# Seven filling matmuls instead of thirteen ahead of the first inverse transform, and two of four weight differences on GpSimd

## The chip, the cores and the metric

The kernel runs on one core of a Trainium2 chip. The core has a matrix engine (TensorE, PE in the profile, with its weight loads as PEld), VectorE (DVE), ScalarE (ACT), GpSimd (POOL) and SyncE (SP, used here only to issue transfers), and 16 DMA engines. The metric is the time of one execution in microseconds on the device, the median of several.

## What is computed

A spectral filter along the sequence, followed by a feed-forward layer with a squared ReLU:

```
X = rfft(x, axis=1)                  # x: 8 x 3008 x 256
y = irfft(X * (filt_r + i filt_i))   # 1505 frequencies x 256 channels
t = y.reshape(24064, 256)
h = max(t @ w_in, 0)                 # w_in:  256 x 2048
out = (h * h) @ w_out                # w_out: 2048 x 256
```

Inputs and output are float32; inside the kernel matmuls take float16 and accumulate in float32.

## The kernel before, in words

**The transform** of each of the 8 sequences is a product of 3008 = 64 x 47 points and takes four matmul steps. `unit_a` makes the 47-point transforms (result u, written to DRAM as dU). `read_u` brings it back turned (ut). `unit_b` makes the 64-point step, and VectorE multiplies it with the filter (prod, L421). For sequences 1 to 7 GpSimd then issues two DMAs per piece that add the swapped half to the other (L429). `unit_p` makes the first inverse step (ze, written to DRAM as dZ). `read_z` reads a quarter of it back as z: two DMAs, one per half of the partitions, into one of two z tiles that take turns (L479). `unit_y` makes the last inverse step: four matmuls (L497), and a copy of PSUM to yt by ScalarE (L504) or VectorE (L506). yt holds channels by tokens.

**The feed-forward layer** works on 47 groups of 512 tokens. The main loop runs over slots s, 8 per group. In each slot `ffn_g1` makes two hidden tiles of 128 x 512 of group g (eight matmuls at most, L527) and ScalarE applies the ReLU (L531); every second slot VectorE squares four tiles (L538).

The second matmul of group g - 1 goes on in the same slots. All groups but the last use seven products of half-size blocks instead of eight. With h cut into a11, a12, a21, a22 (even and odd hidden tiles, first and second half of the tokens) and W_out into b11, b12, b21, b22 (even and odd hidden tiles, left and right 128 columns), `sums` makes four sums of blocks of h per group on VectorE (L613, L616, L619, L622), and `make_t` makes, once in the kernel, four differences of the blocks of W_out, each 128 x 1024 in float16:

- T0 = b12 - b11, used by product 5
- T1 = b22 - T0, used by product 6
- T2 = b22 - b12, used by product 7
- T3 = b21 - T1, used by product 4

`products` spreads the seven products over eight slots (the table PARTS) and collects them in two PSUM tiles psX and psY (matmuls L642). Copies by ScalarE and additions by VectorE (L657, L663) finish the two halves "top" and "bot" of the output, and SyncE stores them.

**The order of work.** Each engine runs its instructions in the order in which the program issues them; the order is written out by hand. In the main loop a slot issues, one after the other: `ffn_g1` of the group, transform units that `fft_plan` puts there, the differences, the products of the group before, more units, the sums, the square, and the stores. Products of group 0 begin in slot 9.

**Around the change.** The prologue handles sequence 0 alone. Its last lines (L790 to L805) read the first two quarters of z. GpSimd copies one element of the first quarter (`tiny`, L793), which makes it wait for z; only then does it issue the two loads of W_out (`load_wout`, L321; 8 of 16 hidden tiles each, turned to float16 on the way). TensorE goes through the 47-point steps of sequence 1 (`unit_a`, L347), whose results SyncE writes to dU (L330), and then through the filling matmuls (L800): products of a zero tile with a constant into a PSUM tile that nothing reads. After them come the first four pieces of `unit_y` (with two zero matmuls each, L495) and the main loop.

The queues that matter here are SyncE's, which holds in this order the writes of dZ, the reads of two quarters of z, the eight writes of dU, the read of z's third quarter (L805), and the read of ut; and GpSimd's, which holds `tiny`, the two loads of W_out, and then nothing until the first DMAs of L429.

Of the kernel before, what the change touches and what calls it, by code (L numbers as in the profile page):

```python
# [110 lines left out]
def kernel(  # L111
# [9 lines left out]
    nc = tc.nc  # L121
# [35 lines left out]
    def psF(name):  # L157
        return pps.tile([128, 512], F32, tag="psF", name=name, bufs=2)
# [316 lines left out]
    def read_z(b, c, ks=(0, 1)):  # L475
        zt = ztiles[c % 2]
        v = dZ[b].rearrange("(q j) d -> q j d", j=NM)
        for k in ks:
            nc.sync.dma_start(out=zt[64 * k:64 * k + 48],  # L479
                              in_=v[48 * k:48 * k + 48, 8 * c:8 * c + 8, :])  # L480
        zts[(b, c)] = zt
# [29 lines left out]
    def ffn_g1(g, s):  # L511
        if s == 0:
            h2s[g] = p_h2.tile([128, NJT, TG], F16, tag="h2", name=f"h2_{g}")
        h2 = h2s[g]
        ps = psH(f"psH_{g}_{s}")
        segs = []
        t = g * TG
        while t < (g + 1) * TG:
            b, r = divmod(t, S)
            n = min((g + 1) * TG - t, S - r)  # L520
            segs.append((t - g * TG, b, r, n))
            t += n
        for i in range(2):
            jt = 2 * s + i
            for o, b, r, n in segs:
                for dt in range(2):
                    nc.tensor.matmul(ps[:, i, o:o + n],  # L527
                                     sWin[:, dt, jt * 128:(jt + 1) * 128],
                                     yts[b][:, dt, r:r + n],
                                     start=(dt == 0), stop=(dt == 1))  # L530
        nc.scalar.activation(out=h2[:, 2 * s:2 * s + 2, :], in_=ps, func=AF.Relu)  # L531

    def ffn_sq(g, s):
        n = 1 if g == NG - 1 else 2
        if (s + 1) % n:
            return
        v = h2s[g][:, 2 * (s + 1 - n):2 * s + 2, :]
        nc.vector.tensor_mul(out=v, in0=v, in1=v)  # L538

    def ffn_g2(g, s):  # L540
        t, half = divmod(s, 2)
        if s % 4 == 0:
            pso[g] = psO(f"psO_{g}_{s}")
        elif g == NG - 1 and half == 0:
            pso[g] = psF(f"psO_{g}_{s}").rearrange("p (a d) -> p a d", d=256)
        for jt in range(8 * half, 8 * half + 8):
            nc.tensor.matmul(pso[g][:, t % 2, :], h2s[g][:, jt, t * 128:(t + 1) * 128],  # L547
                             sWout[:, jt, :], start=(jt == 0), stop=(jt == NJT - 1))

    def ffn_out(g, s):  # L550

        step = 1 if g == NG - 1 else 2
        if (s + 1) % (2 * step):
            return
        n = s // 2 + 1 - step
        ost = p_out.tile([128, 2, 256], F32, tag="ost", name=f"ost_{g}_{s}")
        h0 = n % 2
        nc.scalar.copy(out=ost[:, h0:h0 + step, :], in_=pso[g][:, h0:h0 + step, :])
        store(g, n, step, ost)
# [25 lines left out]
    def make_t(k):  # L585

        w = sWout.rearrange("p (q e) c -> p q e c", e=2)
        b11, b12 = w[:, :, 0, 0:128], w[:, :, 0, 128:256]
        b21, b22 = w[:, :, 1, 0:128], w[:, :, 1, 128:256]
        if k == 0:  # L590
            sg["t"] = p_t.tile([128, 4, 8, 128], F16, tag="t", name="sT")
        t = sg["t"]
        i0, i1 = ((b12, b11), (b22, t[:, 0]), (b22, b12), (b21, t[:, 1]))[k]
        nc.vector.tensor_sub(out=t[:, k], in0=i0, in1=i1)
        sg["w"] = {1: b11, 2: b21, 3: b22, 4: t[:, 3], 5: t[:, 0], 6: t[:, 1], 7: t[:, 2]}

    def quads(g):
# [3 lines left out]
    def sums(g, k):  # L601

        if k not in (0, 1, 2, 4):
            return
        a11, a12, a21, a22 = quads(g)
        if k == 0:
            sg[g] = {1: a11, 2: a12, 4: a22}
        f = sg[g]
        if k in (0, 2):
            f["s"] = p_x32.tile([128, 2, 8, D], F16, tag="x32", name=f"sum_{g}_{k}")  # L610
        t = f["s"][:, 0 if k in (0, 2) else 1]
        if k == 0:
            nc.vector.tensor_add(out=t, in0=a21, in1=a22)  # L613
            f[5] = t
        elif k == 1:
            nc.vector.tensor_sub(out=t, in0=f[5], in1=a11)  # L616
            f[6] = t
        elif k == 2:
            nc.vector.tensor_sub(out=t, in0=a11, in1=a21)  # L619
            f[7] = t  # L620
        else:
            nc.vector.tensor_sub(out=t, in0=a12, in1=f[6])  # L622
            f[3] = t
# [7 lines left out]
    def products(g, k, s):  # L631

        f = sg[g]
        for p, m0, m1 in PARTS[k]:
            if p == 1 and m0 == 0:
                f["x"] = psO(f"psX_{g}").rearrange("p a (t c) -> p a t c", t=2)
            if p == 2 and m0 == 0:
                f["y"] = psO(f"psY_{g}").rearrange("p a (t c) -> p a t c", t=2)
            o = f["x"][:, 0] if p in (1, 6, 7, 4) else f["y"][:, 0 if p == 2 else 1]
            for m in range(m0, m1):  # L640
                q, t = divmod(m, 2)
                nc.tensor.matmul(o[:, t, :], f[p][:, q, 128 * t:128 * t + 128], sg["w"][p][:, q, :],  # L642
                                 start=(m == 0 and p in (1, 2)), stop=(q == 7),
                                 skip_group_check=True)
            if m1 < 16:
                continue
            if p == 1:
                f["top"] = p_out.tile([128, 2, 256], F32, tag="ost", name=f"top_{g}")
                nc.scalar.copy(out=f["top"][:, :, 0:128], in_=o)
            elif p == 6:  # L650
                nc.scalar.copy(out=f["top"][:, :, 128:256], in_=o)
            elif p == 7:
                f["bot"] = p_out.tile([128, 2, 256], F32, tag="ost", name=f"bot_{g}")
                nc.scalar.copy(out=f["bot"][:, :, 128:256], in_=o)
            elif p == 2:
                for v, i in ((f["top"][:, :, 0:128], 0), (f["bot"][:, :, 128:256], 1)):
                    nc.vector.tensor_add(out=v, in0=f["y"][:, i], in1=v)  # L657
            elif p == 4:
                nc.scalar.copy(out=f["bot"][:, :, 0:128], in_=o)
                stores.append((s + 1, g, 2, f["bot"]))  # L660
            elif p == 3:
                v = f["top"][:, :, 128:256]
                nc.vector.tensor_add(out=v, in0=o, in1=v)  # L663
                stores.append((s + 1, g, 0, f["top"]))
# [64 lines left out]
    def run(plan, s, place):  # L729
        for f, *a in plan.get(2 * s + place, ()):  # L730
            f(*a)
# [64 lines left out]
    for c in range(4):  # L796
        unit_a(1, c)
    ps = psF("fill")
    for _ in range(13):
        nc.tensor.matmul(ps, zero, sSB[:, 0:4, :].rearrange("p a b -> p (a b)"),  # L800
                         start=True, stop=True)
    for n in range(4):
# [1 line left out]
    prologue[0] = False  # L804
    read_z(0, 2)  # L805

    SEVEN = range(NG - 1)
    work = fft_plan()

    for s in range((NG + 1) * SLOTS):  # L810
        g, k = divmod(s, SLOTS)
        if g < NG:
            ffn_g1(g, k)
        run(work, s, 0)
        if 8 <= s < 12:
            make_t(s - 8)
        if (s - 1) // SLOTS - 1 in SEVEN:
            products((s - 1) // SLOTS - 1, (s - 1) % SLOTS, s)
        if g > 0 and g - 1 not in SEVEN:
            ffn_g2(g - 1, k)  # L820
        run(work, s, 1)
        if g > 0 and g - 1 not in SEVEN:
            ffn_out(g - 1, k)
        if g - 1 in SEVEN:
            sums(g - 1, k)
        if g < NG:
            ffn_sq(g, k)
        while stores and stores[0][0] <= s:
            _, i, n, ost = stores.pop(0)
            store(i, n, 2, ost)  # L830
# [30 lines left out]
```

## Time and profile before

| quantity | value |
|---|---|
| median of 9 executions | 759.16 us (757.34 to 761.97) |
| the profiled execution | 761.47 us |
| its span, first to last instruction | 759.7 us |
| mean granted TensorE clock | 0.996 |
| busy share: TensorE, VectorE, ScalarE, GpSimd | 97%, 86%, 74%, 25% |
| filling matmuls (L800) | 13, from 45.79 us to about 48.8 us |
| four differences (L594, VectorE) | 62.42, 64.17, 67.04, 68.78 us; 0.68 to 0.69 us each |
| second half of W_out lands | about 62.34 us |

Times in the profile count from the span's start. A row names the engine, the line, the operation, the tile written and the tiles read, and the shape; a bracket at its end holds the time that the engine stood idle just ahead and what released it. The busy time of neighbouring instructions can overlap a little, since an engine begins an instruction before the one ahead of it has fully drained. A matmul's end is modelled. "Granted clock" is the share of TensorE's full clock that its throttle allowed.

### The profile page before, as it was taken

What the parts mean: (1) busy time and instruction counts of PE and PEld (TensorE: products, weight loads), DVE (VectorE), ACT (ScalarE), POOL (GpSimd) and SP (SyncE); (2) the same over time, 40 slices, a digit from 0 to 9 for tenths busy, and PEclk for the clock granted to TensorE, in tenths of its full rate; (3) what the DMA queues carried; (4) which work ended last, traced back from release to release, by engine and by line L of the source; (5) the groups of instructions that cost most, each with busy time, mean ns of one, the idle gap of its engine ahead of it and who ended that gap; (6) DMA issues with size and microseconds to landing.
All of it is one profiled execution on the core that took longest, in us unless ns stands there. A gap on an engine that the chain in (4) does not pass through costs nothing.

```text
span 759.7 us, 20205 instructions
## 1 busy us (share of the span) xinstructions
PE 738.5 (97%) x8511; PEld 536.4 (71%) x8511; DVE 656.5 (86%) x731; ACT 565.1 (74%) x808; POOL 190.8 (25%) x265
## 2 busy tenths in 40 slices
PE   7888999999999999999999999999998999999997
PEld 5545667777677777877678776777767777777776
DVE  5768998899899898989979998999988989888783
ACT  5766788777878777787777778777776777777773
POOL 2810650244222321232304224133311222000000
PEclk9899999999999999999999999999999999999999
DMA  9986898656785557746586547754446333321011
GB/s 350 296 184 183 141 184 225 176 111 120 167 219 121 97 129 172 184 103 136 105 220 127 125 98 141 228 125 102 103 118 185 88 74 95 98 85 42 30 57 57
DMA packets 103491, 106.36 MB, mean 140 GB/s; under 512 B 10352, under 2 KB 93552, under 8 KB 102248
## 3 DMA queue, kind: packets, MB, share of 16 engines
q1 hardware_dynamic: 83960, 81.83, 35.4%
q0 software_dynamic: 19296, 23.05, 21.4%
q8 instruction: 67, 1.10, 0.6%
q10 hardware_dynamic: 144, 0.18, 0.2%
q14 instruction: 24, 0.20, 0.1%
HBM read 57.80 MB, written 48.23 MB: 140 GB/s over the span
## 4 chain that ended last, share of the span: by engine, by line
PE 86%; DMA 5%; DVE 5%; ACT 1%; issue 1%; SPq 1%; POOL 0%; DVEq 0%; ACTq 0%
PE psH L527 39%; PE psX L642 20%; PE psY L642 16%; PE psB L412 3%; PE psY L497 2%; PE psP L461 2%; DMA sWout<-in_moe_w_out_dram 2%; PE psA L347 2%; DMA zt<-dZ 2%; DVE prod L421 1%; DMA prod<-prod 1%; DMA xw<-in_x_dram 1%; PE psO L547 1%; PE psf L286 1%; DVE h L538 1%
## 5 line engine op out<-in xcount | busy, mean ns | idle before, releaser
L531 ACT ACTIVATE h<-psH 128x1024 f16<-128x1024 f32 x376 | 385.3, 1026 | 161.5 <-PE psH L527 160.5
L527 PE MATMUL psH<-yt,sWin 128*128 128x512 f16 (+7 forms) x1728 | 386.8, 351 | 1.2 <-ACT h L531 0.4
L538 DVE TENSOR_TENSOR h<-h 128x2048 f16<-128x2048 f16 (+1 forms) x192 | 229.9, 1198 | 45.6 <-ACT h L531 45.2
L429 POOL DMA_DIRECT2D prod<-prod x168 | 138.7, 968 | 430.5 <-DVE prod L421 428.1
L527 PEld LDWEIGHTS <-sWin 128*128 128x128 f16 x1728 | 149.1, 98 | 90.5 <-issue 3.0
L642 PEld LDWEIGHTS <-sum 128*128 128x128 f16 x2944 | 181.4, 98 | 26.2 <-issue 6.3
L642 PEld LDWEIGHTS <-h 128*128 128x128 f16 x2208 | 135.6, 98 | 25.0 <-issue 5.9
L421 DVE TENSOR_TENSOR prod<-psB,sF 128x1024 f16<-128x1024 f32 x84 | 102.3, 1219 | 11.9 <-PE psB L412 11.8
L642 PE MATMUL psX<-sT,sum 128*128 128x128 f16 x1472 | 104.7, 219 | 0.0
L642 PE MATMUL psY<-sT,sum 128*128 128x128 f16 x736 | 71.2, 219 | 0.0
L642 PE MATMUL psY<-sWout,sum 128*128 128x128 f16 x736 | 56.0, 219 | 1.4 <-DVE bot L657 1.4
L616 DVE TENSOR_TENSOR sum<-sum,h 128x2048 f16<-128x2048 f16 x46 | 56.1, 1220 | 0.8
L642 PE MATMUL psY<-sWout,h 128*128 128x128 f16 x736 | 56.2, 219 | 0.0
L642 PE MATMUL psX<-sT,h 128*128 128x128 f16 x736 | 56.1, 219 | 0.0
L622 DVE TENSOR_TENSOR sum<-h,sum 128x2048 f16<-128x2048 f16 x46 | 56.0, 1217 | 0.0
L619 DVE TENSOR_TENSOR sum<-h 128x2048 f16<-128x2048 f16 x46 | 56.0, 1217 | 0.0
L195 POOL DMA_DIRECT2D x<-in_x_dram x64 | 55.8, 1045 | 0.5 <-PE psA L347 0.5
L613 DVE TENSOR_TENSOR sum<-h 128x2048 f16<-128x2048 f16 x46 | 55.9, 1216 | 0.0
L463 ACT CAST ze<-psP 128x512 f16<-128x512 f32 x84 | 49.2, 585 | 1.5 <-PE psP L461 1.4
L642 PE MATMUL psX<-sWout,h 128*128 128x128 f16 x736 | 48.8, 219 | 0.4 <-DMA sWout<-in_moe_w_out_dram 0.4
L497 PE MATMUL psY<-sC,zt 112*128 112x94 f16 x512 | 42.3, 204 | 3.3 <-DMA zt<-dZ 2.9
L506 DVE CAST yt<-psY 128x376 f16<-128x376 f32 x62 | 33.7, 544 | 13.1 <-PE psY L497 12.9
(77 smaller groups left out, 547.2 us busy)
## 6 DMA issues: line engine op xcount, KB each, us to landing
zt<-dZ SPq DMA_DIRECT2D x64, 192.0 KB
dU<-u SPq DMA_DIRECT2D x56, 192.0 KB
prod<-prod POOLq DMA_DIRECT2D x168, 64.0 KB, 2.8
dZ<-ze SPq DMA_DIRECT2D x28, 384.0 KB
x<-in_x_dram POOLq DMA_DIRECT2D x48, 192.0 KB, 5.1
ut<-dU SPq DMA_DIRECT2D x7, 1024.0 KB
out_dram<-bot SPq DMA_DIRECT2D x32, 128.0 KB
out_dram<-top SPq DMA_DIRECT2D x16, 256.0 KB
```

What stands on the lines that cost most here:

```text
L195: nc.gpsimd.dma_start(out=t[64 * h + p0:64 * h + p1], in_=v[p0:p1, 8 * c:8 * c + 8, :])
L421: nc.vector.tensor_mul(out=prod[:, :, a:a + n, :], in0=ps.rearrange("p (a d) -> p a d", d=D)[:, a:a + n, :].unsqueeze(1) .to_broadcast([12 ...
L429: nc.gpsimd.dma_start(out=prod[64 * i:64 * i + 64, 0], in_=prod[64 - 64 * i:128 - 64 * i, 1], accum_op=mybir.AluOpType.add)
L497: nc.tensor.matmul(ps[:, 94 * jj:94 * jj + 94], zt[:, 4 * (g % 2) + jj, dt * 128:(dt + 1) * 128], sSY, start=True, stop=True)
L527: nc.tensor.matmul(ps[:, i, o:o + n], sWin[:, dt, jt * 128:(jt + 1) * 128], yts[b][:, dt, r:r + n], start=(dt == 0), stop=(dt == 1))
L531: nc.scalar.activation(out=h2[:, 2 * s:2 * s + 2, :], in_=ps, func=AF.Relu)
L538: nc.vector.tensor_mul(out=v, in0=v, in1=v)
L613: nc.vector.tensor_add(out=t, in0=a21, in1=a22)
L616: nc.vector.tensor_sub(out=t, in0=f[5], in1=a11)
L619: nc.vector.tensor_sub(out=t, in0=a11, in1=a21)
L622: nc.vector.tensor_sub(out=t, in0=a12, in1=f[6])
L642: nc.tensor.matmul(o[:, t, :], f[p][:, q, 128 * t:128 * t + 128], sg["w"][p][:, q, :], start=(m == 0 and p in (1, 2)), stop=(q == 7), skip ...
```

## The change

The filling matmuls ahead of the first pieces of `unit_y` go from thirteen to seven. Of the four differences of W_out blocks, T0 and T1 stay on VectorE and T2 and T3 are issued to GpSimd. Their slots change: T0 and T2 are issued in slot 8, T1 and T3 in slot 9, where before slots 8, 9, 10 and 11 took one each. T0 and T1 thus keep their slots. What is computed is the same.

```diff
         t = sg["t"]
         i0, i1 = ((b12, b11), (b22, t[:, 0]), (b22, b12), (b21, t[:, 1]))[k]
-        nc.vector.tensor_sub(out=t[:, k], in0=i0, in1=i1)
+        eng = nc.vector if k < 2 else nc.gpsimd
+        eng.tensor_sub(out=t[:, k], in0=i0, in1=i1)
...
     ps = psF("fill")
-    for _ in range(13):
+    for _ in range(7):
         nc.tensor.matmul(ps, zero, sSB[:, 0:4, :].rearrange("p a b -> p (a b)"),
                          start=True, stop=True)
...
+    MT = {8: (0, 2), 9: (1, 3)}
...
         run(work, s, 0)
-        if 8 <= s < 12:
-            make_t(s - 8)
+        for i in MT.get(s, ()):
+            make_t(i)
```

## The prediction

> **What bounds the kernel now.** The page's table of engines comes first. It says that there is hardly any idle TensorE time to win: 759.7 - 738.5 = 21 us in all.
>
> ```profile
> PE 738.5 (97%) x8511; PEld 536.4 (71%) x8511; DVE 656.5 (86%) x731; ACT 565.1 (74%) x808; POOL 190.8 (25%) x265
> ```
>
> An average doesn't price two edits at 45.8 and 67 us, so the next view is the chain that ended last, from 38 to 92 us. It reads start, length, work:
>
> ```profile
> 43.90 2.87 DMA zt<-dZ
> ...
> 46.83 0.18 POOL tiny L793
> ...
> 47.99 14.35 DMA sWout<-in_moe_w_out_dram
> ...
> 62.42 0.69 DVE sT L594
> ```
>
> The chain leaves TensorE at the landing of z, goes through GpSimd's small copy to the load of W_out, and hangs on that load until 62.34. Neither the fill (L800) nor the first group's matmuls (L527) are on it. From 62.42 it runs along VectorE up to 73.3. Then TensorE's order of events, whose last bracket is the idle time before a piece and its releaser:
>
> ```profile
> 45.79 2.98 PE L800 MATMUL fill<-sSB,zero 128*128 128x512 f16 x13
> ...
> 48.72 0.33 PE L497 MATMUL psY<-sC,zt 112*128 112x94 f16 x4
> ...
> 62.39 0.61 PE L642 MATMUL psX<-sWout,h 128*128 128x128 f16 x8 [0.42 <-DMA sWout<-in_moe_w_out_dram]
> 62.83 1.03 PE L527 MATMUL psH<-yt,sWin 128*128 128x512 f16 x4
> 64.77 0.33 PE L497 MATMUL psY<-sC,zt 112*128 112x94 f16 x4 [0.91 <-DMA zt<-dZ]
> ```
>
> TensorE waits at two transfers in a row: the second half of W_out (62.39), then the third quarter of z (64.77). From there it has no gap up to 72.63. Next, VectorE's and GpSimd's order of events:
>
> ```profile
> 67.04 0.68 DVE L594 TENSOR_TENSOR sT<-sWout 128x1024 f16<-128x1024 f16 x1
> 67.64 1.22 DVE L619 TENSOR_TENSOR sum<-h 128x2048 f16<-128x2048 f16 x1
> 68.78 0.68 DVE L594 TENSOR_TENSOR sT<-sWout,sT 128x1024 f16<-128x1024 f16 x1
> 69.38 0.54 DVE L506 CAST yt<-psY 128x376 f16<-128x376 f32 x1
> 69.84 1.22 DVE L538 TENSOR_TENSOR h<-h 128x2048 f16<-128x2048 f16 x1
> ```
> ```profile
> 47.06 1.83 POOL L321 DMA_DIRECT2D sWout<-in_moe_w_out_dram  x2
> 73.63 1.76 POOL L429 DMA_DIRECT2D prod<-prod  x2 [24.74 <-DVE prod L421]
> ```
>
> VectorE runs without a gap from 62.42 past 73.70; GpSimd has nothing to do from 48.89 to 73.63. Last, three stretches by engine: TensorE's busy us stand first, its granted clock behind POOL's.
>
> ```profile
> 20.00:25.00 5.00, 2.54 (x62) 1.27 (x58) 3.32 (x5) 3.50 (x4) 2.95 (x5) 0.88 1.03 410
> 25.00:30.00 5.00, 5.00 (x62) 2.46 (x63) 4.10 (x4) 3.09 (x3) 4.79 (x10) 0.50 1.07 312
> 60.00:65.00 5.00, 3.67 (x33) 2.07 (x32) 3.80 (x5) 3.51 (x5) 0.00 (x0) 1.00 0.54 149
> ```
>
> A half-busy stretch was followed by half the clock; the one around W_out kept it.
>
> **Part 1, six fills fewer.** The thirteenth fill starts 2.6 us after the first (48.4): 2.6/12 = 0.217 each. Six go: 1.30 us of TensorE. The z matmuls move from 48.72 to 47.42. GpSimd's copy saw z's first row at 46.83; the second half of that read was issued after it and its landing isn't shown. It may cost from 0 to the whole 1.30; I take 0, and under the cover that follows it costs 0 anyway.
>
> Does the 1.30 reach the end? The first group (L527 from 50.17, ReLU, yt, squares) is released by its own members, so it moves earlier as a whole. At 62.39 the wait for W_out grows from 0.42 to 1.72, and VectorE's from 0.99 to 2.29. The landing stays: its issue hangs on GpSimd's copy, thus on z. SP's queue is busy issuing the U writes (L330) from 46.43 to 56.28, whose inputs were cast by 47.65; z's third quarter is issued behind them, at 56.39, and lands at 64.73 whatever TensorE does. So part 1 is hidden by two loads: 0 us. Without that cover it pays up to 1.30 (rival C).
>
> The longer wait has a price of its own. From 60.67 to 64.77 TensorE would work only from 62.39 to 63.86. The clock fell at 23.75 after 3.41 us (20.36 to 23.77) with 1.51 busy, 44%; the thinnest 3.41 us that kept it here, 61.97 to 65.38, had 2.08, 61%. A stretch that starts at 61.30 would have 1.47 now, 43%. So between nothing and the fall of the clock, which took 6.9 us at half (23.75 to 30.6) or 3.4 us of dense matmuls; I take nothing, as the matmuls at 20 us load only 32 columns each, and leave the other end to rival E.
> The Trainium skill, "TensorE: Matmul & The Clock Gate" (Why this matters for your kernels), asks only that no gap exceeds some 3 us. The longest gap before the fall at 23.75 was 1.28 us, so the row is stricter than the page; by the page the price here is 0, by the row up to 3.4.
>
> **Part 2, two differences to GpSimd.** Consecutive starts (67.04 to 67.64, 68.78 to 69.38) make each worth 0.60 to VectorE: 1.20 us go. How much arrives? The yt copy would be done at 68.64, but the square at 69.84 needs ScalarE's ReLU, which ends at 69.61 and hangs on TensorE's unbroken stream. So it starts at 69.66: 0.18 is left, for the sum and product behind it too. The next square starts at 73.70, and its ReLU (72.66 plus 1.02) ended at 73.68: 0.02 is left. The product (74.83), the additions (75.97, 76.30) and the matmul that waits for them (76.77) follow as before. The gain is 0 to 0.2 us; I take 0.
>
> GpSimd's first difference may start at 62.4 with W_out, the second at T1's end, 64.85; their readers are at 70.54 (p = 7) and 73.82 (p = 4). Queued behind them on GpSimd are only prod's accumulating DMAs, at 73.63.
>
> Their duration isn't in the trace. Low end: GpSimd's one-input cast of 128x1024, 1.04 (at 20.98). High end: its f16 copies of 512 took 0.61, so 1.22 for 1024, and two operands in turn 2.44. The copy is nearest in type, and a second operand adds between nothing and a second copy: I take 1.83. They end at 64.25 and 66.7, 6 and 7 us ahead of need.
>
> What do they cost VectorE, which works on SBUF operands all that time? Low end 0: L421 kept its 1.22 beside GpSimd's casts at 35 to 39, though one of its operands is in PSUM. High end: the whole duration. Nearest row: VectorE's cast at 21.77 ran beside GpSimd's (20.98 to 22.02) and took 0.79, where the six of that shape at 5.58 to 11.98 took 0.69: 0.10 lost over 0.25 of overlap, 40%. Taken: 0.4 x 2 x 1.83 = 1.46. Against 1.20 taken off, VectorE ends 0.26 behind. 0.73 of it falls ahead of sum L616, which ends at 65.99 and is needed at 66.91: inside 0.92.
>
> The Trainium skill would charge more: "SBUF — State Buffer" (SBUF: two separate sides) has VectorE with two SBUF inputs and a reading GpSimd instruction lock one another out wholly, and "GPSIMD Engine Reference" (Performance versus the Vector engine) some 2.6 cycles at 1.2 GHz per element, an estimate of 2.2 us each. By these pages the sum would be 2 x 2.2 - 1.2 = +3.2 us; the row at 21.77 shows a loss, but only of a part.
>
> **Sum.** 0 (fills) + 0.3 (VectorE) = +0.3 us. The profiled execution (span 759.7, so 1.77 around it) would go from 761.47 to 761.8. It stands 2.3 us above the median of 759.16, and has one wait for z of 2.00 us at 580.76 that the other sequences lack; I add to the median: 759.5.
>
> **Rivals.**
> B, the lock: VectorE stands still for GpSimd's full time. At 1.04 each, 2.08 - 1.20 = +0.9 us, 760.1; at 2.44 each, 4.88 - 1.20 = +3.7, 762.8. Sum L616 slips past 66.91, p = 6 waits, and the square of 69.84 is late. For: VectorE has no gap from 62.42 to 73.70. Against: the 40%. It makes the kernel slower once VectorE loses 1.5 + 1.2 = 2.7 us, 1.36 for each difference.
>
> C, the loads don't decide in most executions. They were late by 0.42 + 0.91 = 1.33; if they land that much sooner, TensorE's 1.30 arrives whole. VectorE's differences can then start only behind the square of 60.20, at 61.4, 1.0 sooner, while ReLU comes 1.33 sooner: the 0.35 between them is what part 2 takes away. -1.65 us, 757.5; with all of part 2, -2.5, 756.7. For: the executions spread over 4.6 us. Against: the 2.00 us at 580.76 explains most of what lifts this one above the median.
>
> D, GpSimd gets no turn until VectorE reads PSUM (68.2): the first difference is done at 70.0 to 70.6 against 70.54, the second at 73.8 to 74.4 against 73.82. 0 to +0.6 us, 759.2 to 759.8: the edit only moves work.
>
> E, the clock: a thin stretch at 60.7 to 64.8 halves it, and the dense matmuls from 65 on lose 3.4 us: 762.6. For: 43% against the 44% that let it fall. Against: the stretch must lie so; below 44% it does for starts of 60.6 to 61.4, a quarter of 3.41 us.
>
> **How the numbers follow.** Likeliest, hidden with a partial loss, 0.36: its own range, -0.2 to +1.0, is 759.0 to 760.2. B 0.20, of which 0.16 beyond 1.5 us. C 0.22. E 0.18. D 0.04. 0.2% is 1.5 us, about what a measurement of this kernel can tell from no change. Faster: nearly all of C and a stray wait for z that goes, 0.24. Slower: E, B's upper part and a stray wait that comes, 0.37. Within: 0.39. The range takes in most of C, B and E: 756.8 to 762.9.
>
> **What would show it.** Right: seven fills, z matmuls near 47.4, waits for W_out and z still ending at about 62.4 and 64.8, the first some 1.7 long; GpSimd's differences at 1 to 2.4 us, sums beside them at 1.2 to 1.9; the square of 69.84 within 0.5. Wrong towards slower: sums above 2.5 with p = 6 waiting, or a clock under 1.00 between 60 and 72. Wrong towards faster: no wait for W_out, and the matmul of 76.77 earlier by over 1.3.

## The result, and the profile after

The changed kernel is slower: 761.35 us (758.88 to 765.99, 15 executions) against 759.01 (45 executions). The ratio is 1.0034, with a 95% interval of 1.0023 to 1.0044; on 759.0 us that is +2.6 us (+1.7 to +3.3). Forecast were 759.5 us, in a range of 756.8 to 762.9, with no visible change as the likeliest (0.39) and slower next (0.37). The time lies in the range, but the step that should have given it failed: the price of GpSimd's two subtractions to VectorE.

The profiled execution after took 765.99 us, span 764.2, and is the slowest of the fifteen. Its table of engines against the one before (PE 738.5, DVE 656.5, POOL 190.8):

```profile
PE 741.5 (97%) x8505; PEld 538.1 (70%) x8505; DVE 659.1 (86%) x729; ACT 565.1 (74%) x808; POOL 196.4 (26%) x267
```

GpSimd gained 5.6 us for two instructions. VectorE lost two instructions and yet gained 2.6 us of busy time. Where, its order of events shows (start, length, instruction; line numbers after `make_t` are one or two higher than before):

```profile
61.36 0.69 DVE L595 TENSOR_TENSOR sT<-sWout 128x1024 f16<-128x1024 f16 x1 [0.77 <-DMA sWout<-in_moe_w_out_dram]
61.97 3.14 DVE L614 TENSOR_TENSOR sum<-h 128x2048 f16<-128x2048 f16 x1
65.03 0.68 DVE L595 TENSOR_TENSOR sT<-sWout,sT 128x1024 f16<-128x1024 f16 x1
65.63 1.21 DVE L617 TENSOR_TENSOR sum<-sum,h 128x2048 f16<-128x2048 f16 x1
66.77 3.14 DVE L538 TENSOR_TENSOR h<-h 128x2048 f16<-128x2048 f16 x1
69.83 1.21 DVE L620 TENSOR_TENSOR sum<-h 128x2048 f16<-128x2048 f16 x1
70.96 0.54 DVE L506 CAST yt<-psY 128x376 f16<-128x376 f32 x1
71.42 1.21 DVE L538 TENSOR_TENSOR h<-h 128x2048 f16<-128x2048 f16 x1
```

Each instruction has its usual length but two: the sum of 61.97 and the square of 66.77 take 3.14 us where they took 1.22. Before, the same two were:

```profile
63.03 1.22 DVE L613 TENSOR_TENSOR sum<-h 128x2048 f16<-128x2048 f16 x1
...
65.91 1.22 DVE L538 TENSOR_TENSOR h<-h 128x2048 f16<-128x2048 f16 x1
```

Beside the two long ones stand the two moved differences. GpSimd's order of events:

```profile
61.44 2.58 POOL L595 TENSOR_TENSOR sT<-sWout 128x1024 f16<-128x1024 f16 x1 [13.32 <-DMA sWout<-in_moe_w_out_dram]
65.79 3.03 POOL L595 TENSOR_TENSOR sT<-sWout,sT 128x1024 f16<-128x1024 f16 x1 [1.76 <-DVE sT L595]
```

GpSimd starts at 61.44, while VectorE is in T0, and ends at 64.02; the sum ends at 65.11. It starts again at 65.79, while VectorE is in the next sum, and ends at 68.82; the square ends at 69.91. Both times VectorE ends 1.09 us behind GpSimd, which is its own 1.22 less the first 0.13. So VectorE stands still until GpSimd is nearly done, and loses 3.14 - 1.22 = 1.92 us, twice.

From the start of T0 to the start of the square behind the yt copy VectorE now takes 71.42 - 61.36 = 10.06 us. Before it was 69.84 - 62.42 = 7.42. The difference of 2.64 is 2 x 1.92 - 2 x 0.60, to the hundredth, and agrees with the +2.6 of the whole kernel.

TensorE's order of events around the fills and the two loads (the bracket: idle time before, and its releaser):

```profile
44.50 2.89 PE L801 MATMUL fill<-sSB,zero 128*128 128x512 f16 x7
...
61.32 0.61 PE L643 MATMUL psX<-sWout,h 128*128 128x128 f16 x8 [0.19 <-DMA sWout<-in_moe_w_out_dram]
61.76 1.03 PE L527 MATMUL psH<-yt,sWin 128*128 128x512 f16 x4
65.16 0.37 PE L497 MATMUL psY<-sC,zt 112*128 112x94 f16 x4 [2.37 <-DMA zt<-dZ]
```

Two things in this execution need care. First, the seven fills take 2.68 us up to the next matmul's start at 47.18, since the granted clock stood at 0.50 from about 44.8 to 48.2 us. Second, the wait for W_out is 0.19 and the one for z 2.37, and the clock fell again from about 65.3 to 68.7. In the sequence at 580 us z is late once more, and the clock falls behind that wait. Two stretches by engine, with TensorE's busy us first behind the length and its granted clock third from the end:

```profile
580.00:584.00 4.00, 0.77 (x12) 0.46 (x10) 1.19 (x2) 1.09 (x2) 1.64 (x2) 1.00 0.66 153
584.00:588.00 4.00, 4.00 (x37) 3.21 (x35) 2.54 (x3) 1.43 (x2) 0.00 (x0) 0.57 0.24 72
```

That is why this execution stands 4.5 us of span above the profiled one of before, and not 2.6. The square behind the yt copy is 1.58 later (71.42 against 69.84, W_out having landed 1.06 sooner). The wait for z at 580 is 3.23 us against 2.00. And 4 us at a clock of 0.57 cost 1.7. The sum is 4.5. The last two terms aren't needed for the loss: the same kernel profiled again (below) has neither.

### The profile page after: what moved, and what is told of

Read it like the earlier page. It is cut to its first block, busy times and chain, and to the rows that moved or that the text cites. A ratio compares the mean times of both kernels' runs of the same rounds, so it can differ in the third digit from the quotient of the medians.

```text
span 764.2 us, 20194 instructions
## 1 busy us (share of the span) xinstructions
PE 741.5 (97%) x8505; PEld 538.1 (70%) x8505; DVE 659.1 (86%) x729; ACT 565.1 (74%) x808; POOL 196.4 (26%) x267
## 4 chain that ended last, share of the span: by engine, by line
PE 86%; DMA 6%; DVE 4%; ACT 2%; SPq 1%; issue 1%; POOL 0%; DVEq 0%; ACTq 0%
PE psH L527 38%; PE psX L643 20%; PE psY L643 15%; PE psB L412 3%; PE psY L497 2%; PE psP L461 2%; PE psA L347 2%; DMA ut<-dU 2%; DMA zt<-dZ 1%; DMA dU<-u 1%; DVE prod L421 1%; DMA xw<-in_x_dram 1%; PE psO L547 1%; DVE h L538 1%; PE psf L286 1%
## 5 line engine op out<-in xcount | busy, mean ns | idle before, releaser
L421 DVE TENSOR_TENSOR prod<-psB,sF 128x1024 f16<-128x1024 f32 x84 | 102.3, 1219 | 12.8 <-PE psB L412 12.7
L614 DVE TENSOR_TENSOR sum<-h 128x2048 f16<-128x2048 f16 x46 | 57.9, 1258 | 0.0
L620 DVE TENSOR_TENSOR sum<-h 128x2048 f16<-128x2048 f16 x46 | 56.0, 1217 | 0.0
L497 PEld LDWEIGHTS <-zt 112*128 112x128 f16 x512 | 33.2, 98 | 19.5 <-issue 3.7
```

The lines of the kernel that those rows point to most:

```text
L421: nc.vector.tensor_mul(out=prod[:, :, a:a + n, :], in0=ps.rearrange("p (a d) -> p a d", d=D)[:, a:a + n, :].unsqueeze(1) .to_broadcast([12 ...
L497: nc.tensor.matmul(ps[:, 94 * jj:94 * jj + 94], zt[:, 4 * (g % 2) + jj, dt * 128:(dt + 1) * 128], sSY, start=True, stop=True)
```

## The experiments

Each was timed with the kernel before on the same chip, and intervals are those of the ratio. "Stretch" is the time on VectorE from the start of T0 to the start of the square behind the yt copy.

| kernel | stretch, us | ratio to before | us |
|---|---|---|---|
| before | 7.42 | | |
| the change | 10.06 | 1.0034 (1.0023 to 1.0044) | +2.6 |
| the change again | 10.07 | 1.0031 (1.0016 to 1.0046) | +2.4 |
| seven fills alone | 7.42 | 1.0001 (0.9987 to 1.0016) | +0.1 |
| GpSimd alone | 10.07 | 1.0035 (1.0022 to 1.0047) | +2.7 |
| T2 alone on GpSimd | 8.75 | 1.0006 (0.9996 to 1.0016) | +0.5 |
| T2, T3 left out, 13 fills | 6.21 | 0.9988 (0.9974 to 1.0003) | -0.9 |
| T2, T3 left out, 7 fills | 6.21 | 0.9982 (0.9969 to 0.9995) | -1.4 |
| extra GpSimd copies | 9.34 | 1.0032 (1.0021 to 1.0043) | +2.4 |
| extra GpSimd memsets | 7.41 | 1.0002 (0.9989 to 1.0016) | +0.2 |
| sums first, 7 fills | | 0.9990 (0.9980 to 1.0000) | -0.8 |
| differences in halves, 7 fills | | 0.9997 (0.9985 to 1.0010) | -0.2 |
| sums first, z first, 7 fills | | 0.9984 (0.9971 to 0.9997) | -1.2 |
| z first, 13 fills | | 0.9999 (0.9986 to 1.0012) | -0.1 |

The theory after the result was the lock, rival B. Its rivals were the clock (E) and the thought that the fills do the harm. The two parts were taken apart first.

**Seven fills alone.**

```diff
-    for _ in range(13):
+    for _ in range(7):
         nc.tensor.matmul(ps, zero, ...)
```

> Seven fills alone, all four differences on VectorE as before. Theory lock (VectorE stands still while GpSimd subtracts): this edit has no part in the loss; -0.5 to +0.3 us against before, no instruction of L613 or L538 above 1.3 us. Theory clock (the longer wait at W_out and z halves TensorE's clock): +1.5 to +3 us, and a profile with a granted clock of 0.50 behind 64 us. Rival C of the prediction (the loads do not decide): -1.3 us.

Measured: 1.0001, no change (-1.0 to +1.2 us). TensorE's order of events:

```profile
45.91 1.68 PE L800 MATMUL fill<-sSB,zero 128*128 128x512 f16 x7
...
48.77 0.33 PE L497 MATMUL psY<-sC,zt 112*128 112x94 f16 x4 [1.06 <-DMA zt<-dZ]
...
64.26 0.33 PE L497 MATMUL psY<-sC,zt 112*128 112x94 f16 x4 [0.94 <-DMA zt<-dZ]
```

The fills end sooner and TensorE waits for z instead: 1.06 of the 1.30 us are given back at once. So the fills covered a real wait, and the wait for z's third quarter (0.94) follows as before. The harm isn't here, and neither is the gain.

**GpSimd alone.** The change's edit of `make_t` and of its slots, with thirteen fills.

```diff
+        eng = nc.vector if k < 2 else nc.gpsimd
+        eng.tensor_sub(out=t[:, k], in0=i0, in1=i1)
...
+        for i in MT.get(s, ()):
+            make_t(i)
```

> Thirteen fills, T2 and T3 on GpSimd. Theory lock: the two VectorE instructions beside GpSimd's take about 3.1 us instead of 1.2, 2 x 1.9 lost less 1.2 taken off, so +2.6 us, less what a late z covers: +1.8 to +2.6. Theory clock: within 0.5 us of before, as the wait for W_out stays short.

Measured: 1.0035, the whole of the change's loss. VectorE's order of events:

```profile
61.71 3.14 DVE L614 TENSOR_TENSOR sum<-h 128x2048 f16<-128x2048 f16 x1
...
66.51 3.14 DVE L538 TENSOR_TENSOR h<-h 128x2048 f16<-128x2048 f16 x1
```

The same two instructions of 3.14 us. The granted clock was 1.00 in this execution from 44 to 74 us, so the loss doesn't need a slower clock.

**The two differences left out**, with thirteen and with seven fills, to see what VectorE's 1.20 us were worth at most.

```diff
-        sg["w"] = {..., 4: t[:, 3], 5: t[:, 0], 6: t[:, 1], 7: t[:, 2]}
+        sg["w"] = {..., 4: t[:, 1], 5: t[:, 0], 6: t[:, 1], 7: t[:, 0]}
...
-        if 8 <= s < 12:
+        if 8 <= s < 10:
             make_t(s - 8)
```

> Thirteen fills; T2 and T3 are left out (products 7 and 4 take T0 and T1 in their place), so VectorE is rid of two instructions and GpSimd gets none. It shows what the move could have gained at best. The prediction's step: 0 to -0.2 us, since ScalarE's ReLU takes over at 69.6 and 73.7. If VectorE were what bounds that stretch: -1.2 us.

> Seven fills; T2 and T3 left out, products 7 and 4 take T0 and T1. Both gains of the change without GpSimd. If the two loads hide both: -0.5 to 0 us. If the loads do not decide (rival C): -1.65 to -2.5. If the clock decides: +1.5 or more, as for seven fills alone.

Measured: -0.9 us (-2.0 to +0.2) and -1.4 us (-2.4 to -0.4). The second is a gain beyond its interval, so "hidden" is not all of it. VectorE's order of events with thirteen fills:

```profile
59.25 1.22 DVE L538 TENSOR_TENSOR h<-h 128x2048 f16<-128x2048 f16 x1 [0.41 <-ACT h L531]
60.39 0.68 DVE L594 TENSOR_TENSOR sT<-sWout 128x1024 f16<-128x1024 f16 x1
```

T0 follows the square at once: in this execution W_out was there. TensorE had no wait for W_out or z between 59 and 73 us either, and with seven fills the profiled execution looks the same. In both, the chain that ended last runs along VectorE from the square ahead of T0 on (here from 59.25 to 70.09 us). So where the loads come in time VectorE is the bound of this stretch, and its 1.20 us count.

**What of GpSimd shuts VectorE out.** Two extra instructions on GpSimd in the kernel before, started by the end of T0 and of T1. Their output is overwritten by T2 and T3.

```diff
+    def beside(k):
+        nc.gpsimd.tensor_copy(out=tiny, in_=t[0:1, k, 0, 0:1])
+        nc.gpsimd.tensor_copy(out=t[:, 2 + k], in_=<1024 elements of sWout>)
...
+        if 8 <= s < 10:
+            beside(s - 8)
```

In the second kernel `nc.gpsimd.memset(t[:, 2 + k], 0.0)` stands in place of the second copy.

> Before (thirteen fills, all differences on VectorE), with two extra one-input copies of 128x1024 float16 on GpSimd, each behind a one-element copy that waits for T0 or T1; what they write is overwritten by T2 and T3. Theory lock for any read: a VectorE instruction beside each copy grows from 1.2 us by the copy's own duration (1.2 us, twice GpSimd's 0.61 for 512), so +1.5 to +2.4 us. If only two-input subtractions shut VectorE out: 0 us, no VectorE instruction above 1.3 us in the stretch.

> The same with memsets of 128x1024 float16 in place of the copies, so GpSimd writes but hardly reads. Theory lock of the read side: 0 us, VectorE's instructions keep 1.2 us. If any access of GpSimd shuts VectorE out: VectorE grows by the memset's duration (0.5 to 1 us each), +0.5 to +1.5 us.

Measured: the copies +2.4 us (+1.6 to +3.3), the memsets +0.2 (-0.8 to +1.2). With the copies, VectorE and then GpSimd:

```profile
63.45 1.65 DVE L594 TENSOR_TENSOR sT<-sWout,sT 128x1024 f16<-128x1024 f16 x1
...
66.15 2.18 DVE L538 TENSOR_TENSOR h<-h 128x2048 f16<-128x2048 f16 x1
```

```profile
62.53 1.04 POOL L600 COPY tiny<-sT 1x1 f16<-1x1 f16 x1 [14.34 <-DVE sT L594]
63.52 1.03 POOL L601 COPY sT<-sWout 128x1024 f16<-128x1024 f16 x1
65.23 1.05 POOL L600 COPY tiny<-sT 1x1 f16<-1x1 f16 x1 [0.68 <-DVE sT L594]
66.22 1.03 POOL L601 COPY sT<-sWout 128x1024 f16<-128x1024 f16 x1
```

T1 grows from 0.69 to 1.65 and the square from 1.22 to 2.18: 0.96 us each for copies of 1.03. The one-element copies took 1.04 instead of the 0.18 of `tiny`, for they waited in turn for VectorE. With the memsets, VectorE and then GpSimd:

```profile
63.11 0.69 DVE L594 TENSOR_TENSOR sT<-sWout,sT 128x1024 f16<-128x1024 f16 x1
63.71 1.22 DVE L622 TENSOR_TENSOR sum<-sum,h 128x2048 f16<-128x2048 f16 x1
64.85 1.22 DVE L538 TENSOR_TENSOR h<-h 128x2048 f16<-128x2048 f16 x1
```

```profile
63.17 0.94 POOL L601 MEMSET sT<- 128x1024 f16 x1
...
64.91 0.94 POOL L601 MEMSET sT<- 128x1024 f16 x1
```

A memset of 0.94 beside VectorE costs it nothing. It is GpSimd's reading of SBUF that shuts out a VectorE instruction with two SBUF operands. It does so whether GpSimd reads one operand or two, and for nearly as long as GpSimd's instruction runs.

**One difference instead of two.**

```diff
+        eng = nc.gpsimd if k == 2 else nc.vector
+        eng.tensor_sub(out=t[:, k], in0=i0, in1=i1)
...
+        for i in {8: (0, 2), 9: (1,), 11: (3,)}.get(s, ()):
+            make_t(i)
```

> Thirteen fills; only T2 goes to GpSimd, in slot 8; T0, T1 and T3 stay on VectorE in their slots. Theory lock: one sum of 3.1 us, 1.92 lost less 0.60 taken off, half of the whole change: +1.3 us. If only the second subtraction (beside the square, behind T1) did the harm: 0 us.

VectorE's order of events:

```profile
62.82 0.69 DVE L595 TENSOR_TENSOR sT<-sWout 128x1024 f16<-128x1024 f16 x1 [1.46 <-DMA sWout<-in_moe_w_out_dram]
63.42 3.15 DVE L614 TENSOR_TENSOR sum<-h 128x2048 f16<-128x2048 f16 x1
...
71.57 1.21 DVE L538 TENSOR_TENSOR h<-h 128x2048 f16<-128x2048 f16 x1
```

The stretch is 8.75 us, 1.33 longer than before: 1.92 - 0.60, half of the change. The time of the kernel moved by +0.5 us (-0.3 to +1.2), less than the 1.3 expected, though the medians, 760.65 and 759.40, lie 1.25 apart. The lock is as long as expected; how much of it the kernel as a whole shows stays open.

**A better order.** If VectorE bounds the stretch, work that needs no W_out should run while it waits for W_out, or be cut by the two loads.

```diff
-        if 8 <= s < 12:
+        if 9 <= s < 12:
             make_t(s - 8)
...
-        if g - 1 in SEVEN:
+        if g - 1 in SEVEN and s != 9:
             sums(g - 1, k)
+        if s == 8:
+            sums(0, 1)
+            make_t(0)
```

> Seven fills, all differences on VectorE, and the first two sums (which need no W_out) issued ahead of T0, so that VectorE adds while it waits for W_out. If VectorE bounds 62 to 77 us: up to the wait for W_out, 0.8 to 1 us, is gained in executions where W_out comes late, 0 where it comes early: -0.3 to -1 us. If ScalarE and TensorE bound it, as the prediction held: 0.

> Seven fills, all differences on VectorE, each in two halves by the two loads of W_out: the first halves go into slots 6 and 7, where VectorE has gaps of 0.4 to 0.6 us, the second halves where the whole ones were. VectorE bound: four halves of 0.3 us leave the crowded stretch, -1.2 there at a cost of up to 0.4 ahead of it: -0.5 to -1.4 us. If the first half of W_out lands too late for slot 6: 0 or slower.

The halves: `make_t(k, e)` takes four of the eight q; e = 0 in slots 6 and 7, e = 1 where the whole differences stood. Sums first gave -0.8 us (-1.5 to 0.0). The halves gave nothing (-1.1 to +0.8): the first halves pushed the yt copy back, and TensorE waited 1.53 us for it at 60.80.

Then z's third quarter was read ahead of the last two writes of U, with the sums first and alone:

```diff
-        if b == 1:
+        if b == 1 and c < 3:
             write_u(b, c)
...
     read_z(0, 2)
+    write_u(1, 3)
```

> Seven fills and the first two sums ahead of T0, as in the kernel with the sums first, and on SyncE's queue the read of z's third quarter goes ahead of the last two U writes. The third quarter then lands some 2 us sooner, and the wait of 0.7 to 0.9 us for it at 64 us goes; W_out and the turned U come no later, as the bytes are the same: -1 to -2 us against before. If the next wait (VectorE at 69 us) takes its place: no better than -0.8, as with the sums alone.

> Before (thirteen fills, all on VectorE in the old order) with the read of z's third quarter ahead of the last two U writes alone. If the late z quarter is what bounds the stretch: up to the 0.9 us of that wait. If W_out and then VectorE bound it: 0.

Alone it gives nothing (-1.1 to +0.9). With the sums first and seven fills it is the one complete kernel that beat the one before, by 1.2 us (-2.2 to -0.2). Its interval overlaps that of the sums alone, so the order of the reads isn't shown to add anything. TensorE's first wait in it:

```profile
63.62 0.61 PE L642 MATMUL psX<-sWout,h 128*128 128x128 f16 x8 [1.68 <-DMA sWout<-in_moe_w_out_dram]
```

In this execution the wait for z at 64 us was gone as expected, and a longer one for W_out stood in its place.

**The change again**, for an ordinary profile of it.

> The changed kernel once more, for a second profile of it. Theory lock: from T0's start to the square behind the yt copy VectorE takes 10.06 us as in its first profile (before: 7.42), two instructions of 3.1 us, with the clock at 1.00 from 50 to 80 us or not: +2.3 to +2.9 us. Theory clock: where the clock holds at 1.00, no more than +0.5 us is left.

Measured: 1.0031, profiled at 760.3 us. VectorE's order of events, and two stretches by engine:

```profile
60.83 0.69 DVE L595 TENSOR_TENSOR sT<-sWout 128x1024 f16<-128x1024 f16 x1 [0.63 <-DMA sWout<-in_moe_w_out_dram]
61.44 3.14 DVE L614 TENSOR_TENSOR sum<-h 128x2048 f16<-128x2048 f16 x1
...
66.24 3.14 DVE L538 TENSOR_TENSOR h<-h 128x2048 f16<-128x2048 f16 x1
...
70.90 1.21 DVE L538 TENSOR_TENSOR h<-h 128x2048 f16<-128x2048 f16 x1
```

```profile
60.00:70.00 10.00, 8.16 (x88) 5.29 (x87) 9.37 (x7) 6.08 (x10) 5.62 (x2) 1.00 0.66 225
70.00:80.00 10.00, 7.08 (x78) 5.13 (x78) 10.00 (x12) 4.55 (x7) 4.25 (x6) 1.00 0.24 44
```

The stretch is 10.07 us with the clock at 1.00 throughout, and nothing is late at 580 us. The clock is out as the cause.

## Why the prediction was right or wrong, step by step

The time of 761.35 us lies in the forecast range because the range was drawn wide enough for most of rivals B, C and E. The main account gave +0.3 us, with a range of its own up to +1.0, and the change cost +2.6. By the prediction's own sign (sums above 2.5 us, with the product that reads them waiting) its account of part 2 was wrong, and that the time fell into the range is luck for it. Rival B, which had a chance of 0.20, is what happened.

- **Fills hidden by two loads: right, by a different wait.** Seven fills alone change nothing. The term "the second half of that read ... I take 0" was wrong: it cost 1.06 us in the kernel with seven fills alone and 1.13 in the second profile of the change. In those two executions TensorE didn't wait for W_out at all, instead of 1.7 us; in the first profile of the change, whose fills ran at half the clock, it waited 0.19.
- **A fall of the clock, rival E: it happens, but doesn't decide.** In the first profile after, the clock fell at 65.3, behind 3.41 us (61.87 to 65.28) with 1.04 us busy. The stretch was 10.06 us there and 10.07 in two executions at full clock. A wait of 1.68 us for W_out in the kernel with z first didn't let it fall. Nor is the busy share by itself the sign that the prediction took it for: the fall at 44.8 in the first profile after came behind 3.41 us (41.40 to 44.81) with 2.34 us busy, 69%, most of it in matmuls with weights of 47 x 64, more than the 61% that kept the clock before. What decides it stays open.
- **Part 2's gain of 0: too low.** Leaving the two differences out is worth 0.9 to 1.4 us, of which only the second, with seven fills, is beyond its interval. The reasoning from ScalarE's ReLU was read from the profiled execution, in which both loads were late, and no run tests it there; in others (the kernels without T2 and T3) nothing was late and VectorE was the bound. That is the condition of rival C, and I read one execution as all.
- **GpSimd's duration of 1.83 us: right.** 1.92 us of VectorE were lost to each; the records of 2.58 and 3.03 hold a wait for VectorE ahead of that. The estimate of 2.2 us from the Trainium skill, "GPSIMD Engine Reference" (Performance versus the Vector engine), was near as well.
- **"40%" of the overlap: the step that failed.** It is 100%: 2 x 1.92 = 3.84 us lost instead of 1.46, so +2.64 on VectorE instead of +0.26. Rival B's sum, at 1.92, is exactly that, and its condition (1.36 us for each) was met. What was in doubt was read from one row of before, and the row was misread. Here it is, with GpSimd's beside it:

```profile
21.77 0.79 DVE L222 CAST f<-f 128x1024 f16<-128x1024 f32 x1
```

```profile
20.98 1.04 POOL L222 CAST f<-f 128x1024 f16<-128x1024 f32 x1 [3.85 <-DMA f<-in_filt_i_dram]
```

GpSimd ended at 22.02. By what the profile after shows, VectorE ends its own duration less 0.13 behind that: 22.02 + 0.69 - 0.13 = 22.58. The row ended at 22.56. It fits a full lock, seen over its last 0.25 us, part of which VectorE spends on its start anyway. The division 0.10 by 0.25 was no rate.

A longer overlap of the same kind bears this out. In the profile of T2 alone on GpSimd, a load came late and the two engines' casts of 128x1504 ran at the same time (VectorE's row, then GpSimd's):

```profile
17.47 2.03 DVE L222 CAST f<-f 128x1504 f16<-128x1504 f32 x1
```

```profile
17.26 1.44 POOL L222 CAST f<-f 128x1504 f16<-128x1504 f32 x1 [3.71 <-DMA f<-in_filt_r_dram]
```

GpSimd ended at 18.70 and VectorE at 19.50: its usual 0.94 (in the kernel before, with GpSimd done) less 0.13, and 1.09 us lost. With T2 and T3 left out and seven fills the cast took 2.01 in the same way. So a VectorE cast with one SBUF operand is shut out as well as a sum with two.

- **The other row, L421 unharmed at 35 to 39:** right as a row, wrong as an end of the range. L421 has one operand in PSUM and the sums have none.
- **Rival D, GpSimd gets no turn:** fell. It got its turn between two VectorE instructions that stood back to back, and T2 was done at 64.02.
- **0.73 us inside a cover of 0.92:** with 1.92 in its place the cover was gone. In the second profile of the change TensorE waits 0.31 for the first sum, 0.25 for the second and 1.18 for VectorE's yt copy behind them, where before it had no wait for them.

The Trainium skill had this: "SBUF — State Buffer" (SBUF: two separate sides) says that the pair of SBUF ports common to VectorE and GpSimd isn't split but held for the whole instruction, against a VectorE instruction with two SBUF inputs only if GpSimd's reads SBUF. The copies (0.96 lost of 1.03) and the memsets (0 of 0.94) agree with both halves of that. It was set aside in favour of a row that, read with the instruction's start in mind, agrees with it.

## What to carry to other kernels

An engine with idle time isn't free help for its neighbour: before moving elementwise work to GpSimd, look whether VectorE's instructions at that moment take all their operands from SBUF (here the sums, the squares and the casts from float32 to float16) and whether GpSimd's would read SBUF. If so the move costs VectorE nearly GpSimd's full duration (here 1.92 us) to save its own (0.60). A short overlap can't give a rate of loss: line up when both instructions end, not how much longer one took. And where a kernel's executions differ in which load is late, a term "hidden by that load" holds for some of them only; a relief of the engine that is next in line pays in the others.

## What was unexpected in the hardware

- The lock runs both ways, and for tiny reads too: a GpSimd copy of one element took 1.04 us beside VectorE's sums, against 0.18 alone.
- Between back-to-back VectorE instructions the waiting GpSimd gets the next turn: in no profile here did it wait longer than the rest of one VectorE instruction (61.44 to about 62.1, and 65.79 to about 66.9).
- The clock of TensorE changed on a grid: in the first profile after it fell at about 24.3, 44.8 and 65.3 us, 20.5 us or six times 3.41 apart, and came back 3.4 us later each time. The grid lay differently in other executions: the clock fell at 42.7 us with T2 and T3 left out and thirteen fills, and not at all between 31 and 74 us in the profiled execution before.
